# Four output banks behind attention, the last expert by blocks of tokens, and a four-block normalization in one instruction

## The chip, the cores and the metric

The kernel runs on one core of one Trainium2 chip. The metric is the device time of one execution in microseconds (us), inputs in DRAM at the start and the output in DRAM at the end. The engines in the rows are PE (TensorE), DVE (VectorE), ACT (ScalarE), POOL (GpSimd) and SP (SyncE, which issues DMAs here); PSUM is the memory of eight banks that PE writes its sums to.

## The reference

Attention within a window and with 32 global tokens, then a two-layer network over all tokens, then a mixture of eight experts in which each expert takes exactly 272 of the 2176 tokens.

```python
# attention: 4 batches, 8 heads, 512 local + 32 global tokens, 64 per head
# each softmax: exp(s - max) / (sum + 1e-9)
x = attn_out.transpose(0, 2, 1, 3).reshape(2176, 512)
# first network
h = x @ w_in                                        # 512 -> 2048
x = (np.maximum(h, 0) + alpha * np.minimum(h, 0)) @ w_out      # 2048 -> 512
# experts: greedy by the sorted logits, at most 272 tokens each
logits = x @ w_gate
for e in range(8):
    out[mask[e]] = np.maximum(x[mask[e]] @ w1[e], 0) @ w2[e]   # 512 -> 1024 -> 512
```

The weights w_in, w_out, w1 and w2 are used in fp32 accuracy.

## The kernel before

**Numbers.** Nearly all products are made of a fast fp32 format (fp32r in the rows). For accuracy each operand is split into a rounded high half and the rest, and a product is the sum of three: high by high, low by high, high by low. `split` (L73) makes both halves: ACT copies the high one, and DVE or POOL subtracts for the low one. So `g` becomes `ghi` and `glo`, with `glo` on POOL, and an expert's hidden values become `hh` and `hl`. The weights of the first network arrive as 64-bit numbers; `decoding` (L76 to 93) turns them into fp32 on DVE (tile `mag`).

**Stages.** The tokens are in eight chunks of 272 (c = 0 to 7). Features stand on the partitions, tokens along the columns. The hidden 2048 are done in two halves (hf = 0, 1) of eight column blocks (f = 0 to 7).

1. Attention alone, up to about 46 us: PE, DVE and ACT in an order written by hand. A step takes four windows of queries: `scores`, then `norm` (L395 to 401), which adds 1e-9 to the four row sums, takes the reciprocal and scales four blocks of 128 x 128 of P (tile `pr`), then the transposes and the product with v.
2. Attention mixed with the first network, up to about 222 us: the framework's scheduler sets the order. Here `share[0]` is set for a time, and two of the four scalings of a step go to ACT.
3. `gemm` for chunks 3 to 7 of hf = 0, 228 to 357 us, with PE's order as written. In each chunk come eight first products (`gemm1`, 12 matmuls each, tile `h`, epilogue on ACT and at L202 on DVE), then the second product: four output blocks d = 0 to 3, each a sum over eight f with three matmuls for each (L230), tile `y`. A finished bank is copied by ACT to `xd` (L236; two buffers in SBUF), and SP stores it. Beside this the weights of hf = 1 are loaded and decoded.
4. `gemm1b`, the first products of hf = 1, up to about 470 us; then the second products of hf = 1 (L1218) together with the router, which finds each expert's 272 tokens.
5. Eight experts in turn (`slot`): `up` (L1087), `down` (L1105), and `emit`, which transposes the results of the expert before (L1123), copies them to rows and scatters them by token (L1139). The 272 tokens are two blocks of 128 and a rest of 16; the rests of all eight experts are collected in `otail` and scattered at the end as one block of 128.

**What sets the order around the change.** In `gemm` of stage 3 the list at L222 gives PE's order. The banks of `y` come from the pool `pY`, which has two; `gemm1` meanwhile takes its banks `h` in turn from `pH` (two) and, once `odd` is set, from `pO` (two). Between stages 3 and 4 the code puts the router's constants on DVE and POOL (L694 to 779), and behind them `Lrow`, `loadx(0, 1)` and `splitx(0, 1)` (L780 to 782), the load and the split of the first x of stage 4. Each engine runs its own queue in order; the scheduler places instructions of the engines that have no order by hand, so the constants stand in DVE's and POOL's queues in the midst of chunk 7. At the end, `turned` puts the last expert's transposes between the matmuls of `down`, and `emit(E - 1)` follows the last product.

## Time and profile before

| | us |
|---|---|
| three timed runs | 830.79, 832.97, 835.6 |
| their median | 832.97 |
| the profiled execution's own time | 830.71 |
| its span in the trace | 828.933 (shown as 828.9) |
| PE busy | 793.3, 96% of the span |
| DVE, ACT, POOL busy | 472.7, 394.4, 350.6 |

The rows below come from that one profiled execution. In a timeline row stand the start and the duration in us, the engine, the source line, the operation with out<-in, the shapes, the number of like instructions in a row, and in brackets how long the engine had been idle and which instruction released it. Consecutive matmuls overlap in the rows, so the pitch between their starts tells more than the duration of one. The granted clock of PE (PEclk) is a share of the full 2.4 GHz. Idle time of an engine that sets no pace costs nothing.

### The profile page before, as it was taken

How to read it: one execution, taken by the hardware profiler on the slowest of the kernel's cores; microseconds unless marked ns; L12 is line 12 of the kernel's file. 1: busy time of each engine (PE TensorE's matmuls, PEld its weight loads, DVE VectorE, ACT ScalarE, POOL GpSimd, SP SyncE). 2: the span in 40 equal slices, each digit the busy share in tenths (PEclk: the TensorE clock that was granted, in tenths of full speed). 3: DMA queues.
4: the chain of work that ended last, by engine and by line, in shares of the span. 5: the costliest groups of instructions: out<-in, count | busy, mean ns of one | idle time of the engine just before them, and what ended most of it. 6: DMA issues, size and time to landing. Idle time of an engine off the chain costs nothing.

```text
span 828.9 us, 20981 instructions
## 1 busy us (share of the span) xinstructions
PE 793.3 (96%) x8328; PEld 736.8 (89%) x8328; DVE 472.7 (57%) x1681; ACT 394.4 (48%) x982; POOL 350.6 (42%) x305
## 2 busy tenths in 40 slices
PE   7989999999998999899999999999999999999995
PEld 5767778988998999799999999999899999999995
DVE  6899955364267664623334357777677777651120
ACT  6786646564454554323333334342455655454421
POOL 1134322020145443400000465663689989688501
PEclk9999999999998999999999999999999999999998
DMA  9975642631245242003131215424366676466201
GB/s 352 393 286 196 206 151 80 229 130 49 65 151 170 65 129 81 9 21 108 55 108 55 82 53 183 153 58 161 86 203 213 209 219 179 146 193 211 92 27 38
DMA packets 49083, 115.99 MB, mean 140 GB/s; under 512 B 4456, under 2 KB 22312, under 8 KB 46937
## 3 DMA queue, kind: packets, MB, share of 16 engines
q1 hardware_dynamic: 46089, 105.74, 39.4%
q0 software_dynamic: 2896, 8.92, 3.0%
q8 instruction: 65, 1.06, 0.5%
q14 instruction: 33, 0.27, 0.1%
HBM read 96.80 MB, written 17.83 MB: 138 GB/s over the span
## 4 chain that ended last, share of the span: by engine, by line
PE 44%; issue 6%; POOL 3%; DMA 2%; DVE 2%; ACT 1%; POOLq 0%; SPq 0%; ACTq 0%
PE h L196 12%; PE h L1218 10%; PE h L1105 7%; PE h L1087 6%; POOL m L73 2%; DMA raw<-in_moe_w_dram 2%; PE lp L273 1%; PE h L1295 1%; PE pc L923 1%; PE y L230 1%; PE yt L251 1%; PE xt L1067 1%; POOL out_dram L1139 1%; POOL xg L1035 1%; DVE gs L889 0%
## 5 line engine op out<-in xcount | busy, mean ns | idle before, releaser
L196 PE MATMUL h<-xh,win 128*128 128x272 f32 x768 | 161.6, 298 | 2.8 <-ACT win L72 1.2
L73 POOL TENSOR_TENSOR m<-raw,m 128x1024 fp32r<-128x1024 f32 x64 | 152.2, 2398 | 17.3 <-ACT m L72 12.8
L196 PEld LDWEIGHTS h<-xh,win 128*128 128x128 f32 x768 | 125.0, 189 | 11.9 <-issue 4.2
L230 PE MATMUL y<-ghi,wout 128*128 128x272 f32 x512 | 112.6, 303 | 6.7 <-ACT xd L236 2.9
L73 POOL TENSOR_TENSOR glo<-g,ghi 128x272 fp32r<-128x272 f32 x64 | 54.5, 856 | 137.1 <-ACT ghi L72 127.0
L196 PE MATMUL h<-xl,win 128*128 128x272 f32 x384 | 111.3, 290 | 0.0
L73 POOL TENSOR_TENSOR gr<-gb,gr 128x272 fp32r<-128x272 f32 x64 | 47.9, 784 | 148.0 <-ACT gr L72 147.5
L1105 PE MATMUL h<-hh,m 128*128 128x272 f32 x512 | 103.8, 294 | 0.0
L1087 PE MATMUL h<-xsh,m 128*128 128x272 f32 x512 | 103.1, 293 | 0.7 <-DVE hl L1093 0.7
L230 PEld LDWEIGHTS y<-ghi,wout 128*128 128x128 f32 x512 | 85.3, 193 | 13.0 <-issue 3.6
L1218 PE MATMUL h<-gr,wout 128*128 128x272 f32 x672 | 95.1, 294 | 0.0
L201 ACT ACTIVATE neg<-h 128x272 f32<-128x272 f32 x128 | 50.4, 395 | 81.1 <-PE h L196 79.0
L1218 PEld LDWEIGHTS h<-gr,wout 128*128 128x128 f32 x672 | 87.0, 189 | 0.4 <-ACT gr L72 0.4
L72 ACT CAST m<-raw 128x1024 fp32r<-128x1024 f32 x64 | 65.9, 1049 | 41.6 <-DMA raw<-in_moe_w_dram 40.9
L1105 PEld LDWEIGHTS h<-hh,m 128*128 128x128 f32 x512 | 81.5, 188 | 1.5 <-issue 1.5
L1087 PEld LDWEIGHTS h<-xsh,m 128*128 128x128 f32 x512 | 81.6, 188 | 0.9 <-DVE hl L1093 0.9
L230 PE MATMUL y<-glo,wout 128*128 128x272 f32 x256 | 75.5, 296 | 2.8 <-POOL glo L73 2.8
L1105 PE MATMUL h<-hl,m 128*128 128x272 f32 x256 | 75.3, 294 | 0.0
L1087 PE MATMUL h<-xsl,m 128*128 128x272 f32 x256 | 73.9, 292 | 0.0
L196 PEld LDWEIGHTS h<-xl,win 128*128 128x128 f32 x384 | 72.9, 190 | 0.4 <-DVE xl L73 0.4
L202 DVE SCALAR_TENSOR_TENSOR g<-neg,al,h 128x272 f32<-128x272 f32 x64 | 35.7, 560 | 59.1 <-ACT neg L201 51.0
L389 ACT ACTIVATE pr<-sc,mx 128x128 f32<-128x128 f32 x128 | 49.9, 392 | 31.2 <-DVE mx L387 31.2
(262 smaller groups left out, 1538.7 us busy)
## 6 DMA issues: line engine op xcount, KB each, us to landing
raw<-in_moe_w_dram SPq DMA_DIRECT2D x64, 512.0 KB, 3.9
vv<-in_v_dram SPq DMA_DIRECT2D x16, 1024.0 KB, 5.9
qk<-in_qk_dram SPq DMA_DIRECT2D x14, 720.0 KB, 8.4
raw<-in_moe_w_in_dram SPq DMA_DIRECT2D x16, 512.0 KB, 7.6
raw<-in_moe_w_out_dram SPq DMA_DIRECT2D x16, 512.0 KB, 5.9
xs<-xb SPq DMA_DIRECT2D x16, 272.0 KB, 6.9
xpart<-xd SPq DMA_DIRECT2D x32, 136.0 KB, 2.2
xb<-xs SPq DMA_DIRECT2D x8, 544.0 KB
```

The lines of the kernel that those rows point to most:

```text
L72: a = A.copy(hi, src)
L73: return a, (lo_eng or V).tensor_tensor(lo, src, hi.bitcast(F32), op=OP.subtract)
L196: T.matmul(ps, wi[:, w, k, fs], x[:, k], start=i == 0, stop=i == 3 * KD - 1)
L201: A.activation(out=neg, in_=ps, func=AF.Relu, scale=-1.0)
L202: epi[0] = V.scalar_tensor_tensor(g, neg, al1[:, hf * KH + f:hf * KH + f + 1], ps, op0=OP.mult, op1=OP.add)
L230: T.matmul(ps, wo[:, w, f, ds_], x[:, f], start=f == 0 and i == 0, stop=f == KH - 1 and i == 2)
L251: T.transpose(t[:, k * 128:(k + 1) * 128], xo[:, k, a:b], ident)
L273: T.matmul(lp[r:r + 32], w, x, start=n < 4, stop=n >= LT - 4)
L389: A.activation(out=d["pr", j][:, ii], in_=sc, func=AF.Exp, bias=d["mx", j][:, ii:ii + 1], scale=-1.0, accum_out=d["sm", j][:, ii:ii + 1])
L1087: T.matmul(ps, d["w1"][:, w, kk, f * 128:(f + 1) * 128], x[:, kk], start=kk == 0 and i == 0, stop=kk == KD - 1 and i == 2)
L1105: T.matmul(ps, d["w2"][:, w, f, ms], x[:, f], start=i == 0, stop=i == 3 * K3 - 1)
L1218: T.matmul(ps[j], wo[:, w, f, ds_], x, start=f == 0 and a == 0, stop=f == KH - 1 and a == 2)
```

## The change

It has three parts; a move of code (1b) goes with the first.

1. **Banks.** In `gemm`, once `odd` is set (chunks 3 to 7), each of the four output blocks has a bank of its own: d = 0 and 1 from `pY` as before, d = 2 from `pH`, d = 3 from `odd[0]`. All four blocks are summed over f = 0 to 5, and then all four over f = 6 and 7. Before, only d = 0 and 1 were split in this way, and d = 2 and 3 followed whole in the same two banks. In 1b `splitx` also returns its DVE instruction, and `Lrow`, `loadx(0, 1)` and `splitx(0, 1)` stand ahead of the router's constants, which are issued under `tc.issue_after` of that split.
2. **The last expert.** Its second product is made by `by_row`: the hidden values are the stationary operand, the weights the moving one, so that tokens stand on the partitions of the sum, two blocks of 128 tokens and 24 matmuls of 512 columns each. The last 16 tokens are done in plain fp32, with weights `m2f` loaded for them alone and 32 columns of hidden values copied by ACT in `up` (tile `otl`), on four strips of 32 rows that a further matmul with `pick` sums up. No transposes follow. The rests of experts 0 to 6 are emitted with expert 6.
3. **Normalization.** In `norm` the four scalings are one two-operand instruction of 128 x 512, with the reciprocals broadcast; where `share[0]` is set, it takes two blocks, and ACT takes two as before.

```diff
...
-        split(xh, xl, X[c, hf][0] if hf else XB[c // CPB][:, :, (c % CPB) * CH:(c % CPB + 1) * CH])
+        st = split(xh, xl, X[c, hf][0] if hf else XB[c // CPB][:, :, (c % CPB) * CH:(c % CPB + 1) * CH])
         X[c, hf] += [xh, xl]
+        return st[1]
...
-    ybank = [pY, "y"]
...
         if (c + 1, hf) in X:
             splitx(c + 1, hf)
         ys = {}
-        for d, fs in [(0, range(KH - 2)), (1, range(KH - 2)), (0, range(KH - 2, KH)), (1, range(KH - 2, KH))] + [
-                (d, range(KH)) for d in range(2, KD)]:
+        most, rest = range(KH - 2), range(KH - 2, KH)
+        if odd:
+            parts2 = [(d, x) for x in (most, rest) for d in range(KD)]
+        else:
+            parts2 = [(d, x) for x in (most, rest) for d in range(2)] + [(d, range(KH)) for d in range(2, KD)]
+        for d, fs in parts2:
             if d not in ys:
-                ys[d] = ybank[0].tile([128, CH], F32, name="y", tag=ybank[1])
+                pool, tag = (pY, "y") if d < 2 or not odd else (pH, "h1") if d == 2 else odd[0]
+                ys[d] = pool.tile([128, CH], F32, name="y", tag=tag)
             ps = ys[d]
             ds_ = slice(d * 128, (d + 1) * 128)
             for f in fs:
...
             sm = G[p]["sm", j]
             V.tensor_scalar(sm, sm, 1e-9, None, op0=OP.add)
             V.reciprocal(sm, sm)
-            for ii in range(4):
-                x, r = G[p]["pr", j][:, ii], sm[:, ii:ii + 1]
-                if ii % 2 and share[0]:
-                    A.mul(x, x, r)
-                else:
-                    at_norm[p, j] = V.tensor_scalar(x, x, r, None, op0=OP.mult)
+            pr = G[p]["pr", j]
+            own = slice(0, 4, 2 if share[0] else 1)
+            x = pr[:, own]
+            at_norm[p, j] = V.tensor_tensor(x, x, sm[:, own].unsqueeze(2).to_broadcast(list(x.shape)), op=OP.mult)
+            if share[0]:
+                for ii in (1, 3):
+                    A.mul(pr[:, ii], pr[:, ii], sm[:, ii:ii + 1])
 
         def ptrans(p, j):
             d = G[p]
...
-        ybank[:] = [p4, "h4"]
...
+        Lrow = gx2.tile([128, LR], F32, name="Lrow")
+        loadx(0, 1)
+        quiet = ExitStack()
+        quiet.enter_context(tc.issue_after(splitx(0, 1).ins))
...
             P.memset(vas[i], 0.0)
             sbs.append(rc_.tile([128, NP, 32], BF, name=f"sbs{i}"))
             P.memset(sbs[i], 0.0)
-        Lrow = gx2.tile([128, LR], F32, name="Lrow")
-        loadx(0, 1)
-        splitx(0, 1)
+        quiet.close()
...
                                 yield 0.113
                 if kks[-1] == KD - 1:
                     A.activation(out=hh[:, f], in_=ps, func=AF.Relu)
+                    if k == E - 1:
+                        A.activation(out=d["o"][:, f], in_=ps[:, CAP - 32:], func=AF.Relu)
                     V.scalar_tensor_tensor(hl[:, f], ps, 0.0, hh[:, f].bitcast(F32), op0=OP.max, op1=OP.subtract)
                     yield 0.113
...
                     i += 1
                     if i < 3 * K3:
                         yield 0.113
-            if k < E - 1:
-                A.copy(d["o"][:, m], ps)
-            else:
-                A.copy(d["o"][:, m, :256], ps[:, :256])
-                V.tensor_copy(tail["o"][:, m, 16 * k:], ps[:, 256:])
+            A.copy(d["o"][:, m], ps)
 
         scat = []
 
-        def turned(k, m):
-            d = SLOT[k]
-            for q, (a, b) in enumerate(SEG):
-                if m == 0:
-                    pool, tag = ((px, "tx"), (pm, "sm"), (pm, "sm"))[q]
-                    d["t", q] = pool.tile([128, DM], F32, name="ox", tag=tag)
-                T.transpose(d["t", q][:, m * 128:(m + 1) * 128], tail["o"][:, m] if q == 2 else d["o"][:, m, a:b], ident)
+        def scatter(rows, ids):
+            st = P.indirect_dma_start(
+                out=out, out_offset=bass.IndirectOffsetOnAxis(ap=ids, axis=0), in_=rows, in_offset=None)
+            for o in scat:
+                tc.declare_no_dep(st.ins, o.ins, reason="rows of other tokens")
+            scat.append(st)
 
         def emit(k):
             d = SLOT[k]
             orow = sl.tile([128, 3, DM], F32, name="orow")
-            if k < E - 1:
-                A.copy(tail["o"][:, :, 16 * k:16 * k + 16], d["o"][:, :, 256:])
-            for q, (a, b) in enumerate(SEG[:3 if k == E - 1 else 2]):
-                if ("t", q) in d:
-                    t = d["t", q]
-                else:
+            A.copy(tail["o"][:, :, 16 * k:16 * k + 16], d["o"][:, :, 256:])
+            for q, (a, b) in enumerate(SEG[:3 if k == E - 2 else 2]):
+                n = 16 * (E - 1) if q == 2 else 128
+                t = px.tile([128, DM], F32, name="ox", tag="tx")
+                for m in range(KD):
+                    T.transpose(t[:n, m * 128:(m + 1) * 128], tail["o"][:, m] if q == 2 else d["o"][:, m, a:b], ident)
+                A.copy(orow[:n, q], t[:n])
+                scatter(orow[:n, q], TID[:n] if q == 2 else IDS[:, k, q:q + 1])
+                yield 0.5
+
+        def by_row(k):
+            d = SLOT[k]
+            pick = sl.tile([128, 16], F32, name="pick")
+            V.tensor_reduce(pick, ident.rearrange("p (g c) -> p c g", c=32)[:, 16:], axis=AX.X, op=OP.add)
+            orow = sl.tile([128, 3, DM], F32, name="orow")
+            part = d["o"][:, K3:].rearrange("p a b -> p (a b)")
+            terms = [(w, f, x) for f in range(K3) for w, x in ((0, d["h"][0]), (0, d["h"][1]), (1, d["h"][0]))]
+
+            def rows(q, pool, tag):
+                a, b = SEG[q]
+                ps = pool.tile([128, DM], F32, name="ox", tag=tag)
+                for i, (w, f, x) in enumerate(terms):
+                    T.matmul(ps, x[:, f, a:b], d["w2"][:, w, f], start=i == 0, stop=i == len(terms) - 1)
+                    yield 0.22
+                A.copy(orow[:, q], ps)
+                scatter(orow[:, q], IDS[:, k, q:q + 1])
+
+            yield from rows(0, pH, "h1")
+            ps = p4.tile([128, DM], F32, name="ox", tag="h4")
+            for f in range(K3):
+                r = 32 * (f % 4)
+                T.matmul(ps[r:r + 32], d["o"][:, f], d["w2f"][:, f], start=f < 4, stop=f >= K3 - 4)
+            A.copy(part, ps)
+            for i, x in enumerate(rows(1, pH, "h1")):
+                if i == 6:
                     t = px.tile([128, DM], F32, name="ox", tag="tx")
-                    for m in range(KD):
-                        T.transpose(t[:, m * 128:(m + 1) * 128], d["o"][:, m, a:b], ident)
-                (V.tensor_copy if ("t", q) in d and q == 1 else A.copy)(orow[:, q], t)
-                ids = TID if q == 2 else IDS[:, k, q:q + 1]
-                st = P.indirect_dma_start(
-                    out=out, out_offset=bass.IndirectOffsetOnAxis(ap=ids, axis=0), in_=orow[:, q], in_offset=None)
-                for o in scat:
-                    tc.declare_no_dep(st.ins, o.ins, reason="rows of other tokens")
-                scat.append(st)
-                yield 0.5
+                    T.matmul(t[:16], pick, part, start=True, stop=True)
+                    V.tensor_copy(orow[:16, 2], t[:16])
+                    scatter(orow[:16, 2], IDS[:16, k, 2:3])
+                yield x
 
         def slot(k):
             d = SLOT[k]
             d["h"] = (sl.tile([128, K3, CAP], F32R, name="hh"), sl.tile([128, K3, CAP], F32R, name="hl"))
             em = emit(k - 1) if k else iter(())
+            if k == E - 1:
+                d["o"] = sl.tile([128, K3 + DM // 32, 32], F32, name="otl", tag="ot")
             f = 0
             if k == 0:
                 yield from up(k, (0, 1), range(KD - 1), (0, 2))
...
                 if f % 2 == 0:
                     yield next(em, 0)
             d["up"] = True
-            d["o"] = sl.tile([128, KD, CAP], F32, name="ot")
+            if k == E - 2:
+                SLOT[k + 1]["w2f"] = wa.tile([128, K3, DM], F32, name="m2f", tag="wa1")
+                w2e = w2[bass.ds(SLOT[k + 1]["er"], 1)].rearrange("e (k p) f -> p (e k) f", p=128)
+                nc.sync.dma_start(out=SLOT[k + 1]["w2f"], in_=w2e)
+            if k < E - 1:
+                d["o"] = sl.tile([128, KD, CAP], F32, name="ot")
             if k == 0:
-                tail["o"] = sl.tile([128, KD, 128], F32, name="otail", bufs=1)
+                tail["o"] = sl.tile([128, KD, 16 * (E - 1)], F32, name="otail", bufs=1)
+            if k == E - 1:
+                yield from by_row(k)
+                return
             for m in range(KD):
-                for i, x in enumerate(down(k, m)):
-                    if k == E - 1 and m and i == 15:
-                        turned(k, m - 1)
-                    yield x
+                yield from down(k, m)
                 yield 0.113
-            if k == E - 1:
-                turned(k, KD - 1)
...
-        for _ in emit(E - 1):
-            pass
```

PE's order in chunk 3 of stage 3, before, where the first two blocks' sums over f = 0 to 5 end (`y_3911` is d = 1, `y_3882` d = 0, `wout` the weights):

```order
L230 MATMUL y_3911<-ghi_3595,wout_77 128x272 x2
L230 MATMUL y_3911<-glo_3596,wout_77 128x272
L230 MATMUL y_3911<-ghi_3595,wout_77 128x272
L230 MATMUL y_3882<-ghi_3595,wout_77 128x272
L230 MATMUL y_3882<-glo_3596,wout_77 128x272
L230 MATMUL y_3882<-ghi_3595,wout_77 128x272 x2
L230 MATMUL y_3882<-glo_3596,wout_77 128x272
L230 MATMUL y_3882<-ghi_3595,wout_77 128x272
L230 MATMUL y_3911<-ghi_3595,wout_77 128x272
L230 MATMUL y_3911<-glo_3596,wout_77 128x272
```

And after (`y_3821` is d = 1, `y_3840` d = 2):

```order
L235 MATMUL y_3821<-glo_3509,wout_77 128x272
L235 MATMUL y_3821<-ghi_3508,wout_77 128x272 x2
L235 MATMUL y_3821<-glo_3509,wout_77 128x272
L235 MATMUL y_3821<-ghi_3508,wout_77 128x272
L235 MATMUL y_3840<-ghi_3508,wout_77 128x272
L235 MATMUL y_3840<-glo_3509,wout_77 128x272
L235 MATMUL y_3840<-ghi_3508,wout_77 128x272 x2
L235 MATMUL y_3840<-glo_3509,wout_77 128x272
L235 MATMUL y_3840<-ghi_3508,wout_77 128x272 x2
```

Behind f = 5 of d = 1 came f = 6 and 7 of d = 0; now f = 0 of d = 2 comes there.

DVE's order in chunk 7, before, ahead of an epilogue at L202 (`fr`, `home`, `fr_b`, `ones`, `pq_f`, `cols` and `jt` are constants of the router):

```order
L697 TENSOR_SCALAR late<-fr,ipf 128x128
L713 CAST home<-fr 128x17
L720 CAST pq_f<-pq_i 128x2
L724 TENSOR_SCALAR fr_b<-fr 128x128
L733 MEMSET ones 128x128
L735 MEMSET one_c 128x34
L745 TENSOR_SCALAR jt_5362<-j_5360 128x64
L715 TENSOR_SCALAR home<-fr 128x16
L722 TENSOR_SCALAR own<-cols,pq_f 128x24
L202 SCALAR_TENSOR_TENSOR g<-neg,al_70,h_5130 128x272
```

And after (`xl` is the low half of the first x of stage 4, `ipf` and `cols` the first of those constants):

```order
L147 TENSOR_REDUCE wop<-wt 128x4x8
L1351 MEMSET yr 1x512
L837 MEMSET late_pos 128x3
L202 SCALAR_TENSOR_TENSOR g<-neg,al_70,h_5040 128x272
L202 SCALAR_TENSOR_TENSOR g<-neg,al_70,h_5065 128x272
L73 TENSOR_TENSOR xl<-xb,xh 128x1088
L702 CAST ipf<-ip 128x1
L720 CAST cols<-fr 128x24
L722 CAST home<-fr 128x17
L726 TENSOR_SCALAR pq_i<-ip 128x1
```

The constants stood ahead of the epilogue; now the two epilogues and the split of x are ahead of the constants.

PE's order at the end of the kernel, before (`m_11343` is the last expert's w2, `hh` and `hl` the halves of its hidden values, `ot` and `otail` results to be transposed with `ident`):

```order
L1105 MATMUL h_11859<-hl,m_11343 128x272
L1105 MATMUL h_11859<-hh,m_11343 128x272 x2
L1123 MATMUL ox<-ident,ot 128x128 x2
L1123 MATMUL ox<-ident,otail 128x128
L1105 MATMUL h_11859<-hl,m_11343 128x272
L1105 MATMUL h_11859<-hh,m_11343 128x272 x2
L1105 MATMUL h_11859<-hl,m_11343 128x272
L1105 MATMUL h_11859<-hh,m_11343 128x272 x2
L1105 MATMUL h_11859<-hl,m_11343 128x272
L1105 MATMUL h_11859<-hh,m_11343 128x272
L1123 MATMUL ox<-ident,ot 128x128 x2
L1123 MATMUL ox<-ident,otail 128x128
```

And after, at the seam between the two blocks of tokens (`m_11253` is the last expert's w2):

```order
L1154 MATMUL ox<-m_11253,hl 128x512
L1154 MATMUL ox<-m_11253,hh 128x512
L1163 MATMUL ox<-m2f,otl 32x512 x8
L1154 MATMUL ox<-m_11253,hh 128x512
L1154 MATMUL ox<-m_11253,hl 128x512
L1154 MATMUL ox<-m_11253,hh 128x512 x2
L1154 MATMUL ox<-m_11253,hl 128x512
L1154 MATMUL ox<-m_11253,hh 128x512 x2
L1168 MATMUL ox<-otl,pick 16x512
L1154 MATMUL ox<-m_11253,hl 128x512
```

The transposes between and behind the products are gone; the strips of the last 16 tokens stand between the two blocks, and PE's last instruction is a product.

## Rows read from the trace of the kernel before

**Rows 1.** The page: busy us of each engine, share, instructions.

```profile
PE 793.3 (96%) x8328; PEld 736.8 (89%) x8328; DVE 472.7 (57%) x1681; ACT 394.4 (48%) x982; POOL 350.6 (42%) x305
```

**Rows 2.** Timeline of PE, second products of chunks 3 to 6.

```profile
230.70 0.39 PE L230 MATMUL y<-glo,wout 128*128 128x272 f32 x1 [0.40 <-POOL glo L73]
...
252.98 0.29 PE L230 MATMUL y<-ghi,wout 128*128 128x272 f32 x1
...
259.63 0.40 PE L230 MATMUL y<-glo,wout 128*128 128x272 f32 x1 [1.45 <-POOL glo L73]
...
262.30 0.59 PE L230 MATMUL y<-ghi,wout 128*128 128x272 f32 x1 [1.39 <-ACT xd L236]
...
290.80 0.39 PE L230 MATMUL y<-ghi,wout 128*128 128x272 f32 x1 [0.81 <-ACT xd L236]
...
319.71 0.39 PE L230 MATMUL y<-ghi,wout 128*128 128x272 f32 x1 [0.68 <-ACT xd L236]
```

**Rows 3.** Stretches: window, us, each engine's busy us (instructions), PEclk, DMA, GB/s.

```profile
60.00:80.00 20.00, 18.43 (x261) 14.18 (x254) 19.76 (x52) 13.29 (x39) 8.69 (x9) 1.00 0.52 165
260.00:264.00 4.00, 2.61 (x15) 2.39 (x14) 3.86 (x6) 1.85 (x4) 1.27 (x1) 0.67 1.01 307
264.00:268.00 4.00, 4.00 (x20) 4.00 (x19) 0.59 (x1) 0.65 (x2) 1.28 (x1) 0.50 0.88 301
340.00:352.00 12.00, 8.72 (x63) 7.87 (x62) 8.19 (x25) 3.21 (x7) 5.41 (x9) 1.00 0.04 12
780.00:820.00 40.00, 39.54 (x317) 39.13 (x316) 6.26 (x16) 9.27 (x23) 2.25 (x3) 1.00 0.04 14
```

**Rows 4.** Timeline of DVE, POOL and PE in chunk 7.

```profile
338.80 4.80 DVE L202 SCALAR_TENSOR_TENSOR g<-neg,al,h 128x272 f32<-128x272 f32 x1
...
342.48 0.63 POOL L779 MEMSET sbs<- 128x640 bf16 x1
...
344.13 0.76 POOL L73 TENSOR_TENSOR glo<-g,ghi 128x272 fp32r<-128x272 f32 x1 [1.02 <-ACT ghi L72]
...
340.43 0.29 PE L230 MATMUL y<-ghi,wout 128*128 128x272 f32 x1
```

**Rows 5.** Timeline of PE, ACT and POOL from the last expert's second product on.

```profile
806.15 0.29 PE L1105 MATMUL h<-hh,m 128*128 128x272 f32 x1
...
811.20 0.38 PE L1123 MATMUL ox<-ident,ot 128*128 128x128 f32 x2
...
811.45 0.37 PE L1105 MATMUL h<-hl,m 128*128 128x272 f32 x1
...
819.87 0.44 PE L1123 MATMUL ox<-ident,ot 128*128 128x128 f32 x2 [0.46 <-ACT ot L1112]
...
820.23 1.07 ACT L1137 COPY orow<-ox 128x512 f32<-128x512 f32 x2 [0.42 <-PE ox L1123]
...
823.64 0.97 POOL L1139 DMA_INDIRECT out_dram<-orow,TID  x1 [0.30 <-issue]
```

**Rows 6.** Tile `xd`, issue to landing; SP's waits: waited for, total us, times, longest.

```profile
DMA to landing us min/median/max: 1.7/2.2/5.2
...
SPq L79 <- DVE mag L92: 96.5, 23, 8.6
```

**Rows 7.** Plain fp32 on four strips, L140: timeline, then durations in ns, min/median/max.

```profile
332.85 1.07 PE L140 MATMUL wp<-wts,ag 128*32 128x512 f32 x8
...
L140 PE MATMUL wp<-wts,ag x16: 592/604/617, 307.4 to 333.3; 128*32 128x512 f32 x16
```

**Rows 8.** DVE: timeline of three instructions, and durations (ns) of the split of x.

```profile
31.87 0.68 DVE L90 SCALAR_TENSOR_TENSOR mag<-raw,mag 128x512 int32<-128x512 int32 x1
...
32.88 0.88 DVE L401 TENSOR_SCALAR pr<-pr,sm 128x128 f32<-128x128 f32 x4
...
65.81 2.43 DVE L401 TENSOR_SCALAR pr<-pr,sm 128x128 f32<-128x128 f32 x4
...
L73 DVE TENSOR_TENSOR xl<-xb,xh x12: 1278/1294/2376, 41.5 to 434.2; 128x1088 fp32r<-128x1088 f32 x12
```

## The prediction

> **What bounds the kernel now.** I read the busy line first: TensorE (PE) is busy 793.3 of 828.9 us [rows 1]. A faster side engine therefore buys time only where PE waits, so I went through the span in stretches and asked three things of each: does PE wait, for whom, and at which clock. Four places matter for this change.
>
> The first is the second product behind attention: five token chunks, c = 3 to 7. PE waits for the low halves `glo` from POOL and for the copies `xd` on ACT that free a bank: 0.40, 1.45, 1.39, 0.81 and 0.68 us [rows 2]. In chunk 4 the two waits stand 2.7 us apart, and right behind them the granted clock falls to its lower level, 1.2 instead of 2.4 GHz: 0.67 on the average of 260 to 264 us, 0.50 from 264 to 268 [rows 3]. In chunk 7 PE is busy 8.72 of the 12 us from 340 to 352 [rows 3], so 3.28 us are idle, in four waits for `ghi` and `glo` of the last column blocks of h.
>
> The cause of that last loss is one stretch on DVE. The router's constants are queued ahead of the epilogue of f = 5 (L202). That L202 is shown 4.80 us long, to 343.60, and the row of POOL memsets for the router ends at 343.11 [rows 4].
>
> The second place is the end. The last product matmul ends at 819.41, and then come an ACT copy, three transposes, a copy to SBUF, three scatters one behind the other (the last starts at 823.64 and takes 0.97 us) and the landing, up to 828.93: 9.52 us without a product [rows 5].
>
> The third is attention's front, up to about 112 us, where DVE is busy 19.76 of 20 us from 60 to 80 us [rows 3] and PE is fed late. The fourth, from 357 us to the end of the experts, is nearly solid PE and is not touched.
>
> **Part 1, four banks.** In chunks 3 to 7 the pieces now run as d = 0, 1, 2, 3 over f = 0 to 5, then d = 0 to 3 over f = 6 and 7. No matmul is added. A piece over six f is 18 matmuls. A matmul of 272 columns comes every 0.126 us: 40 of them between 806.15 and 811.20 us [rows 5]. So f = 6 is first needed 72 matmuls after the second product begins instead of 36: 9.1 us instead of 4.5. In chunk 4, the worst, that product begins at 252.98 and `glo` of f = 6 lets PE go at 259.63 [rows 2], 6.65 us in. That is inside 9.1, so this wait goes, and so do the smaller ones. The wait for `xd` goes because d = 2 and d = 3 no longer need the banks of d = 0 and 1. Removed: 0.40 + 1.45 + 1.39 + 0.81 + 0.68 = 4.73 us.
>
> With the two waits of chunk 4 gone I expect no fall of the clock there. Its price: 35 matmuls in the 8 us from 260 to 268 [rows 3], of which 1.39 idle; at 0.126 they need 4.4 us, so 8 - 1.39 - 4.4 = 2.2 us.
>
> What is late next: the four `xd` copies now fall 0.76 us apart (6 matmuls) at the chunk's end and share two SBUF buffers, so the third waits for the landing of the first one's store, 1.7 to 5.2 us, median 2.2 [rows 6]. The next chunk's f = 0 and 1 use the other two banks; f = 2 needs that of d = 2 some 24 matmuls, 3.0 us, after the chunk's end. The first copy is done about 1.9 us before that end, so at the median landing the third starts 0.3 us behind the end, in time; at the longest it starts 3.3 us behind it, and with its own 0.4 or so (two copies of twice the width take 1.07 [rows 5]) PE loses 0.7. I put 0.5 us for all five chunks, bounds 0 and 4.
>
> **Part 1b, the constants.** The diff also puts the router's constants on DVE behind the split of the next x, which itself stands behind f = 5 and 6. Then L202 of f = 5 runs at once. But the POOL memsets keep their place ahead of `glo` of f = 5: they end at 343.1, a `glo` takes 0.76 [rows 4], so it is there at 343.9. PE needs it 17 matmuls into the second product, which begins at 340.43 [rows 4]: at 342.5. A wait of 1.4 us is left of the 3.28, a gain of 1.9. Should L202 itself be what POOL holds up, the gain is nothing.
>
> Part 1 in sum: 4.73 + 2.2 + 1.9 - 0.5 = 8.3 us, bounds 3 and 10.
>
> **Part 2, the last expert.** Before: 96 matmuls and nine of the transposes, from 806.15 to 819.41, 13.26 us. After: two blocks of 24 matmuls of 512 columns, 8 plain fp32 matmuls of 512 columns on strips of 32 rows for the last 16 tokens, and one that sums the strips. No row has a 512-column matmul of the fast format. From below it takes its 512 columns at 2.4 GHz, 0.213 us; from above 0.126 x 512/272 = 0.237. I take 0.226: 0.126 us are 302 cycles at the full clock, 30 more than the columns, and that remainder is more likely one per instruction. 48 x 0.226 = 10.8 us. Four plain fp32 matmuls of the same shape on four strips (L140, two instructions each) take 1.07 us [rows 7]: two rounds are 2.1. The summing matmul is one such alone: between a quarter of 1.07 and all of it; one instruction alone is shown as 0.604 [rows 7] and it has two, so I take 0.9. Sum 13.8, 0.55 us more; from 0.7 less to 1.1 more. The tail rows of experts 0 to 6 are now transposed inside the last up product: three transposes take 0.25 us of the stream [rows 5], four about 0.35.
>
> The end gets shorter. Behind the last matmul: a copy of about 0.55 us (two take 1.07), 0.30 to the scatter, 0.97, and from the end of the last scatter's issue to the span's end 4.32 as before [rows 5]: 6.2 instead of 9.52, 3.3 less. The two other scatters go out during the 4 us of matmuls ahead of that. Eight small ACT copies and the 2 MB load of the plain weights go beside the last products: ACT is busy 9.27 of 40 us there and DMA moves 14 GB/s [rows 3]; without that cover the load would cost several us, but it has over 25. Net: 3.3 - 0.55 - 0.35 = 2.4 us, bounds 1.6 and 3.9.
>
> **Part 3, normalization.** Where nothing disturbs DVE, the four instructions of 128 columns take 0.88 us; a two-tensor instruction of 512 columns takes 0.68 [rows 8]. So 0.2 us is saved per step. Some ten steps stand up to 46 us and some six up to 112, where DVE sets the pace: at most 16 x 0.2 = 3.2. The first ones wait for loads and for ACT's exp too, so I take 1.2. Later steps lie under solid PE and give nothing. The scheduler also shuffles PE, ACT and DVE a little between 46 and 120 us, for which I have no row: bounds 4 lost and 5 gained.
>
> The four small instructions cost 0.2 us each, mostly whatever their width. The Trainium skill ("VectorE: DVE Perf Modes", section "The perf-mode tier table") gives fp32 tensor_scalar in SBUF twice the rate of tensor_tensor, which speaks against this edit. By that rule alone the edit would be a loss; the 0.68 us row does not bear it out at this width.
>
> **Sum.** 8.3 + 2.4 + 1.2 = 11.9 us off the profiled execution's 830.71 us: 818.8. That execution lies at the lower end of the three timed runs (830.79 to 835.6, median 832.97), so I add about half of the 2.3 us between them: **820 us**.
>
> **The rivals.**
> A, the copies take the place of the wait: the four bunched `xd` hold ACT, and with it the next chunk's epilogues, about 1 us in each of five chunks. For it: landings up to 5.2 us. Against: the median of 2.2. Part 1 gives 3.8 instead of 8.3: 824.5.
> B, normalization gets slower. A two-tensor instruction may wait for POOL: the split of x takes 1.278 us at best and 2.376 at worst [rows 8]. At 1.1 us more in each of the six steps up to 112 us, 6.6 are lost and 1.2 not gained: 828. Against: the four small ones lose as much already, 2.43 instead of 0.88 us at 65.81 [rows 8]. Half the rate without any waiting, 1.76 us instead of 0.88 in those six steps, would be 826.5; that is what the page's rule makes of it.
> C, slower than before: the store of the first `xd` stands behind a weight load on SP's queue, which waits for decoding on DVE, at the longest 8.6 us [rows 6]. ACT then stands still, and the four banks with it; the next f = 2 comes 9.3 us late. Twice that and two falls of the clock at 2.2: 820 + 23 = 843. It decides from about 6 us of lateness in two chunks on. Against: in the new order ACT's casts of the weights that free those loads stand ahead of the copies.
> D, the change doesn't do what it says: the clock falls in chunk 4 anyway, or the waits only move; 826 to 830.
>
> **How the numbers follow.** The forecast has 0.64 (with a range of its own of 813 to 826), A 0.14, B 0.10, D 0.08, C 0.04. The range 812 to 829 takes in the bounds of parts 2 and 3, A and most of B and D, and leaves C out. Half a per cent, about what a measurement here can tell from no change, is 4.2 us: below 828.8 is faster. Faster 0.86, same 0.10, slower 0.04.
>
> **What will show it.** Right: no PE wait for `xd` and none over 0.2 us for `glo` in chunks 3 to 6, a clock of 1.00 throughout them, one wait of 1 to 2 us in chunk 7; about 0.226 us between the 512-column matmuls and 6.2 us from the last of them to the end. Wrong: ACT's `xd` waiting for DMA with PE idle in f = 2 of the next chunk; a normalization that takes over 0.9 us on average; or new waits of PE between 46 and 120 us, where only the schedule has moved.

## The result, and the profile after

The changed kernel takes 825.5 us (median of 4 runs, 822.52 to 826.96) against 832.25 us before (4 runs): a ratio of 0.9905, with a 95% interval of 0.9878 to 0.9932. A second set, 6 runs against 11, gives 0.9887 (0.9865 to 0.9909). So it is faster, as forecast and inside the range of 812 to 829, but by 7 to 10 us and not by the 12 that lie between the forecast 820 and the median before. The 825.5 also lies nearer to rival A's 824.5 than to the forecast.

The profiled execution took 825.84 us, its span is 824.1. The page's busy line, to be read against [rows 1]: PE does as much as before; DVE lost 15.6 us that the time does not show.

```profile
PE 792.1 (96%) x8290; PEld 732.8 (89%) x8290; DVE 457.1 (55%) x1588; ACT 394.0 (48%) x988; POOL 354.8 (43%) x306
```

**Behind attention.** Timeline of PE, every wait of over 0.12 us from the second product of chunk 3 to that of chunk 7; these rows answer to [rows 2, 4].

```profile
234.29 0.39 PE L235 MATMUL y<-glo,wout 128*128 128x272 f32 x1 [0.33 <-POOL glo L73]
...
274.14 0.39 PE L196 MATMUL h<-xh,win 128*128 128x272 f32 x1 [2.07 <-ACT xd L241]
...
286.66 0.40 PE L235 MATMUL y<-glo,wout 128*128 128x272 f32 x1 [1.09 <-POOL glo L73]
...
343.43 0.39 PE L235 MATMUL y<-glo,wout 128*128 128x272 f32 x1 [1.46 <-POOL glo L73]
```

Of the waits in [rows 2] four are gone and one of 0.33 us stays. Two are new, 2.07 us for a copy `xd` ahead of the next chunk's f = 2, and 1.09 us for `glo` in chunk 5. Chunk 7 keeps one wait of 1.46 us. The stretches that answer to [rows 3] (window, us, busy us of each engine, PEclk, DMA share, GB/s):

```profile
260.00:264.00 4.00, 4.00 (x34) 4.00 (x33) 4.00 (x5) 1.64 (x4) 3.88 (x3) 1.00 0.42 131
264.00:268.00 4.00, 4.00 (x34) 4.00 (x33) 3.86 (x6) 0.76 (x2) 1.36 (x2) 1.00 0.88 269
340.00:352.00 12.00, 10.54 (x84) 10.32 (x83) 6.30 (x34) 2.19 (x4) 4.88 (x8) 1.00 0.01 1
```

In chunk 4 the clock stays up: 68 matmuls in the 8 us in which 35 ran before.

**The end.** Timeline of PE, ACT and POOL from the last expert's second product on, answering to [rows 5]:

```profile
803.38 0.40 PE L1154 MATMUL ox<-m,hh 128*128 128x512 f32 x1
...
808.70 0.40 PE L1154 MATMUL ox<-m,hh 128*128 128x512 f32 x1
809.03 1.92 PE L1163 MATMUL ox<-m2f,otl 128*32 128x512 f32 x16
810.88 0.50 PE L1154 MATMUL ox<-m,hh 128*128 128x512 f32 x1
...
812.70 1.03 PE L1168 MATMUL ox<-otl,pick 128*16 128x512 f32 x2
813.66 0.50 PE L1154 MATMUL ox<-m,hl 128*128 128x512 f32 x1
...
817.45 0.40 PE L1154 MATMUL ox<-m,hh 128*128 128x512 f32 x1
...
817.88 0.58 ACT L1156 COPY orow<-ox 128x512 f32<-128x512 f32 x1 [6.25 <-PE ox L1154]
...
818.74 0.98 POOL L1123 DMA_INDIRECT out_dram<-orow,IDS  x1 [3.17 <-ACT orow L1156]
```

Twenty-four matmuls of 512 columns take from 803.38 to 808.70, 0.231 us from start to start. The last ends at 817.85, and 6.22 us later the kernel ends; before it was 9.52 us. The product itself takes 14.47 us instead of 13.26.

**The front.** Here the profile after is slower: the second product of chunk 3 begins at 231.78 instead of 228.12 us. Whether the change did that was the first question for the experiments.

To compare executions I cut each profile at the same four points: the start of the second product of chunk 3, that of chunk 7, the last matmul into `y`, and the end of the span. The last column is the time at the lower clock before 120 us, summed over stretches of 4 us as (1 - PEclk) x 2 x 4. The names are those of the experiments below.

| kernel | chunk 3 begins | to chunk 7 | chunk 7 | to the end | low clock before 120 |
|---|---|---|---|---|---|
| before | 228.12 | 112.31 | 16.58 | 471.9 | 3.4 |
| changed | 231.78 | 108.01 | 13.97 | 470.3 | 13.6 |
| before_again | 228.94 | 110.97 | 16.61 | 473.1 | 3.4 |
| after_again | 232.16 | 107.95 | 13.96 | 469.9 | 13.6 |
| no_norm | 230.80 | 107.72 | 14.00 | 471.6 | 10.3 |
| no_banks | 230.56 | 111.42 | 14.24 | 469.5 | 10.2 |
| no_row | 230.01 | 107.98 | 13.96 | 472.3 | 10.3 |
| no_const | 229.30 | 107.82 | 16.37 | 471.6 | 3.4 |
| xd4 | 228.75 | 105.74 | 13.97 | 471.5 | 6.9 |
| mem_late | 229.83 | 107.98 | 12.23 | 471.8 | 10.3 |
| xd4_mem | 227.85 | 105.66 | 12.24 | 472.1 | 3.4 |
| phase1 | 230.90 | 107.93 | 12.24 | 470.9 | 10.2 |
| phase2 | 232.15 | 107.14 | 12.23 | 469.7 | 13.6 |
| xd4_mem_old_norm | 230.03 | 105.79 | 12.24 | 470.0 | 6.9 |

The second and third columns of times answer each question on their part to a few tenths of a us, as long as the clock stays up there; in chunk 7 it fell for 3.4 us in before_again and in no_const. The first and the last move by 4 and 3 us between executions of like code.

The runs come in sets, each on a chip of its own together with runs of before, and the medians of before differ: 834.79 us with after_again, no_norm, no_banks and no_row; 833.12 with no_const, xd4, mem_late and xd4_mem; 833.83 with phase1 and phase2; 832.89 with xd4_mem_old_norm. Inside a set I compare times, between sets the ratios to before. The changed kernel's is 0.9887 (0.9905 in the first, smaller set), and the 95% interval of each ratio reaches 0.002 to 0.004, or 2 to 3 us, to either side.

### The profile page after: what moved, and what is told of

Same layout as the page of the kernel before. It is cut to its first block, busy times and chain, and to the rows that moved or that the text cites. A ratio compares the mean times of both kernels' runs of the same rounds, so it can differ in the third digit from the quotient of the medians.

```text
span 824.1 us, 20827 instructions
## 1 busy us (share of the span) xinstructions
PE 792.1 (96%) x8290; PEld 732.8 (89%) x8290; DVE 457.1 (55%) x1588; ACT 394.0 (48%) x988; POOL 354.8 (43%) x306
## 3 DMA queue, kind: packets, MB, share of 16 engines
q8 instruction: 65, 1.06, 0.5%
## 4 chain that ended last, share of the span: by engine, by line
PE 73%; DVE 8%; POOL 5%; issue 5%; DMA 5%; ACT 3%; SPq 0%; POOLq 0%; DVEq 0%; ACTq 0%
PE h L196 20%; PE h L1250 10%; PE y L235 10%; PE h L1094 8%; PE h L1114 7%; PE o L424 3%; DMA raw<-in_moe_w_dram 2%; POOL m L73 2%; PE s L386 2%; PE go L473 2%; PE lp L278 1%; PE t L413 1%; PE h L1327 1%; DVE mag L92 1%; PE pc L930 1%
## 5 line engine op out<-in xcount | busy, mean ns | idle before, releaser
L235 PE MATMUL y<-ghi,wout 128*128 128x272 f32 x512 | 108.6, 298 | 3.1 <-POOL wout L73 2.2
L1114 PE MATMUL h<-hh,m 128*128 128x272 f32 x448 | 91.4, 295 | 0.0
L235 PEld LDWEIGHTS y<-ghi,wout 128*128 128x128 f32 x512 | 82.9, 189 | 8.1 <-issue 3.8
L1114 PEld LDWEIGHTS h<-hh,m 128*128 128x128 f32 x448 | 71.4, 189 | 0.9 <-issue 0.9
L1114 PE MATMUL h<-hl,m 128*128 128x272 f32 x224 | 65.9, 294 | 0.0
L202 DVE SCALAR_TENSOR_TENSOR g<-neg,al,h 128x272 f32<-128x272 f32 x64 | 31.5, 493 | 58.8 <-ACT neg L201 51.9
L202 DVE SCALAR_TENSOR_TENSOR gb<-neg,al,h 128x272 f32<-128x272 f32 x64 | 31.2, 495 | 58.7 <-ACT neg L201 58.7
```

What stands on the lines that cost most here:

```text
L202: epi[0] = V.scalar_tensor_tensor(g, neg, al1[:, hf * KH + f:hf * KH + f + 1], ps, op0=OP.mult, op1=OP.add)
L235: T.matmul(ps, wo[:, w, f, ds_], x[:, f], start=f == 0 and i == 0, stop=f == KH - 1 and i == 2)
L1114: T.matmul(ps, d["w2"][:, w, f, ms], x[:, f], start=i == 0, stop=i == 3 * K3 - 1)
```

## The experiments

### The two kernels once more

The changed kernel, unedited:

> The changed kernel once more, unedited. In the first profile of it the second product of chunk 3 begins 3.67 us later than before (231.91 against 228.24 us). Theory 1, this is chance of one execution (a load of qk that landed 1.65 us later, and falls of the clock whose place is not fixed): the start of chunk 3 is now elsewhere by a microsecond or more, 228 to 231, and the time is 822 to 826. Theory 2, it comes from the new order of instructions between 46 and 120 us: chunk 3 begins at 231.5 to 232.5 again, with falls of the clock at about 58 to 64 and 92 to 97 us.

It took 824.88 us (6 runs), and chunk 3 began at 232.16 us with the clock low for as long as in the first profile. Taken alone this looked like theory 2. The other kernels with the same code up to there say otherwise: they begin chunk 3 anywhere from 227.85 to 232.16, by and large later where the clock was low for longer (last column of the table). The same stretch in two of them, after_again and then xd4_mem:

```profile
60.00:64.00 4.00, 4.00 (x49) 3.51 (x48) 3.81 (x8) 2.60 (x8) 2.02 (x3) 0.50 0.80 326
64.00:68.00 4.00, 4.00 (x30) 3.31 (x29) 2.46 (x5) 0.91 (x2) 1.61 (x1) 0.65 0.41 133
```

```profile
60.00:64.00 4.00, 4.00 (x54) 3.13 (x52) 3.93 (x7) 2.05 (x7) 2.85 (x3) 1.00 0.80 295
64.00:68.00 4.00, 4.00 (x48) 3.45 (x44) 3.55 (x13) 3.50 (x12) 2.05 (x2) 1.00 0.46 144
```

The fall of the clock around 60 us comes in some executions and not in others. The kernel before, unedited, for a second profile:

> The kernel before once more, unedited, for a second profile. Its first profiled execution (830.71 us) lies under the median of all its runs, and there the second product of chunk 3 begins at 228.12 us; in the seven other kernels with the same code up to that point it begins anywhere from 227.85 to 232.16, later where the clock is low for longer between 46 and 100 us. Theory 1, that spread is chance of the execution in the kernel before as well: here chunk 3 begins later by up to 4 us if the clock is low for more than the 3.4 us (weighted) of the first profile, and the time from there to the end stays within 1.5 us of 600.8. Theory 2, the kernel before always reaches chunk 3 at about 228.1.

One run: 831.42 us, chunk 3 at 228.94 with 3.4 us of low clock, and 600.7 us from there to the end. So the rest is steady, but both profiles of before show a good front, and their times lie under the medians of its other runs, 832.25 to 834.79. Theory 1 is not shown by this run; it is borne out by no_norm below, which has the old front, shows the early fall as well (0.50 from 52 to 56 us) and begins chunk 3 at 230.80.

### The four banks

Two banks again, the constants left where the change put them:

```diff
-        if odd:
-            parts2 = [(d, x) for x in (most, rest) for d in range(KD)]
-        else:
-            parts2 = [(d, x) for x in (most, rest) for d in range(2)] + [(d, range(KH)) for d in range(2, KD)]
+        parts2 = [(d, x) for x in (most, rest) for d in range(2)] + [(d, range(KH)) for d in range(2, KD)]
...
-                pool, tag = (pY, "y") if d < 2 or not odd else (pH, "h1") if d == 2 else odd[0]
-                ys[d] = pool.tile([128, CH], F32, name="y", tag=tag)
+                ys[d] = pY.tile([128, CH], F32, name="y", tag="y")
```

> The changed kernel with the second product of chunks 3 to 7 in two banks as before; the router's constants stay behind the split of x. From the start of chunk 3's second product to that of chunk 7's the kernel before takes 112.4 us and the changed one 108.0. Theory 1, four banks alone make that difference: 4.4 us slower than the changed kernel, about 830, with the clock at 0.50 again for some 5 us in chunk 4, behind two waits of 1.4 us. Rival, the fall of the clock in chunk 4 is chance and not of the waits: the clock stays up, and the kernel is 1.5 us slower, 827.

827.64 us, 2.8 more than the changed kernel, and 3.4 more from chunk 3 to chunk 7, where 4.4 were expected. Its timeline of PE and the stretches of chunk 4:

```profile
261.98 0.39 PE L231 MATMUL y<-glo,wout 128*128 128x272 f32 x1 [1.44 <-POOL glo L73]
264.65 0.60 PE L231 MATMUL y<-ghi,wout 128*128 128x272 f32 x1 [1.41 <-ACT xd L237]
```

```profile
260.00:264.00 4.00, 1.80 (x13) 1.36 (x11) 3.93 (x5) 0.98 (x2) 1.92 (x2) 1.00 0.57 172
264.00:268.00 4.00, 3.35 (x15) 3.35 (x16) 2.83 (x3) 2.19 (x5) 1.61 (x2) 0.57 1.07 375
```

The two waits are back and so is the fall of the clock behind them, here for 3.4 us. Chunk 4 (from its second product to that of chunk 5) takes 29.0 us; it was 30.2 in the first profile of before with 6.8 us of low clock, and 28.9 in the second with 3.4. So 3.4 us at the lower clock cost 1.3 here. The fall came behind these two waits in all three profiles that have them. In the eleven profiles with four banks the clock fell in chunk 4 once, behind a wait of 2.06 us; seven others with one wait of 1.06 to 2.07 us in that chunk show no fall there. So the two waits brought it about here, and a single one mostly did not.

### The constants

The constants ahead of the split of x again:

```diff
-        Lrow = gx2.tile([128, LR], F32, name="Lrow")
-        loadx(0, 1)
-        quiet = ExitStack()
-        quiet.enter_context(tc.issue_after(splitx(0, 1).ins))
...
-        quiet.close()
+        Lrow = gx2.tile([128, LR], F32, name="Lrow")
+        loadx(0, 1)
+        splitx(0, 1)
```

> The changed kernel with the router's constants ahead of the split of x again, as before. The second product of chunk 7 takes 16.33 us before and 13.84 in the changed kernel. Theory 1, the place of the constants on DVE makes that difference: 2.5 us slower than the changed kernel, 828, and PE waits for ghi of f = 5. Rival, the four banks alone shorten chunk 7 because f = 6 and 7 are needed later: 0 to 0.8 us slower.

Chunk 7 takes 16.37 us, 2.4 more, and PE waits for `ghi` again:

```profile
340.80 0.39 PE L235 MATMUL y<-ghi,wout 128*128 128x272 f32 x1 [1.63 <-ACT ghi L72]
341.64 0.39 PE L235 MATMUL y<-glo,wout 128*128 128x272 f32 x1 [0.45 <-POOL glo L73]
```

The clock fell here too (the same columns as in the stretches above):

```profile
340.00:344.00 4.00, 2.75 (x13) 2.54 (x14) 3.86 (x20) 2.02 (x4) 1.52 (x2) 0.77 0.00 1
344.00:348.00 4.00, 4.00 (x28) 4.00 (x28) 1.01 (x4) 0.42 (x1) 0.77 (x1) 0.81 0.00 0
```

So the 2.4 us are not all waiting. Without waits chunk 7 takes 12.23 us (mem_late, below). In the changed kernel and in the first profile of before, where the clock stays up, a wait costs its row and 0.27 us more (13.97 less 12.23 and 1.46; 16.58 less 12.23 and 3.27, over four waits). By that estimate the two waits of no_const make 0.9 of its 2.4 us and the fall of the clock 1.5. Of waiting alone the rival's 0 to 0.8 us is thus not far off: with four banks the two waits at f = 7 (0.75 and 0.45 us in the first profile of before) are gone whatever the constants do. What speaks for theory 1 is no_banks: two banks, the constants moved, a full clock in chunk 7, and 14.24 us there, 2.3 less than in the first profile of before, whose clock is full there as well.

The median, 825.52 us, is 0.9913 of before's (0.9887 to 0.9940), 2.2 us more than the changed kernel by ratio where 2.5 were expected, but the two intervals overlap. Medians of six to nine runs do not resolve 2 us of this kernel, and the stretches do.

### The last expert

`up`, `down`, `turned`, `emit` and `slot` as before, with the closing loop over `emit(E - 1)`:

```diff
...
-            if k == E - 1:
-                yield from by_row(k)
-                return
             for m in range(KD):
-                yield from down(k, m)
+                for i, x in enumerate(down(k, m)):
+                    if k == E - 1 and m and i == 15:
+                        turned(k, m - 1)
+                    yield x
...
```

> The changed kernel with the last expert's second product, transposes and scatters as before. In the two profiles the stretch from the end of the logits' transposes (473.28 and 470.00 us) to the end is 355.65 us before and 354.10 in the changed kernel: 1.55 us slower than the changed kernel, about 827. Rival, as forecast, 2.4 us slower: 828.

825.68 us, 0.8 more, with chunk 3 at 230.01. From the last `y` to the end it takes 472.3 us; the three profiles with the old end take 471.9 to 473.1 there, the eleven with the new one 469.5 to 472.1, mean 470.8. The difference of the means is 1.6 us, near the 1.55 expected. Shorter stretches say it without that spread. From the start of the last expert's second product to the end it takes 22.78 or 22.79 us in the three profiles with the old end and 20.68 to 20.70 in the eleven with the new one, 2.09 less. The up product ahead of it, which now has the four transposes of the rests inside, takes 13.42 us instead of 12.99. It starts here, in the first profile of before and then of the changed kernel:

```profile
793.16 0.30 PE L1087 MATMUL h<-xsh,m 128*128 128x272 f32 x1
```

```profile
789.96 0.30 PE L1094 MATMUL h<-xsh,m 128*128 128x272 f32 x1
```

So 1.66 us are left, 0.7 less than forecast; the rival falls.

### The normalization

The four scalings again:

```diff
-            pr = G[p]["pr", j]
-            own = slice(0, 4, 2 if share[0] else 1)
-            x = pr[:, own]
-            at_norm[p, j] = V.tensor_tensor(x, x, sm[:, own].unsqueeze(2).to_broadcast(list(x.shape)), op=OP.mult)
-            if share[0]:
-                for ii in (1, 3):
-                    A.mul(pr[:, ii], pr[:, ii], sm[:, ii:ii + 1])
+            for ii in range(4):
+                x, r = G[p]["pr", j][:, ii], sm[:, ii:ii + 1]
+                if ii % 2 and share[0]:
+                    A.mul(x, x, r)
+                else:
+                    at_norm[p, j] = V.tensor_scalar(x, x, r, None, op0=OP.mult)
```

> The changed kernel with the four scalings of the normalization as before. Theory 1, the new instruction takes 0.69 instead of 0.88 us and saves some 0.2 us in each step that DVE paces: this kernel is 0.5 to 2 us slower than the changed one, 826 to 827.5. Theory 2, the edit costs more by the order it brings between 46 and 230 us than it saves: this kernel is 2 to 4 us faster, 821.5 to 823.5, and chunk 3's second product begins at 228 to 229 us.

825.16 us: 0.3 more, and neither theory's number. DVE spends 35.1 us on the 122 scalings here and 21.3 on the one-instruction form in the changed kernel (groups of instructions by line and shape, of no_norm and then of the changed kernel: count | busy us, mean ns | idle before):

```profile
L406 DVE TENSOR_SCALAR pr<-pr,sm 128x128 f32<-128x128 f32 x122 | 35.1, 348 | 0.9
```

```profile
L404 DVE TENSOR_TENSOR pr<-pr,sm 128x512 f32<-128x512 f32 x29 | 20.0, 689 | 0.7
L404 DVE TENSOR_TENSOR pr<-pr,sm 128x256 f32<-128x256 f32 x3 | 1.3, 420 | 0.1
```

Why 14 us off DVE bring so little shows between 88 and 93 us. DVE, POOL and PE of the changed kernel there, and POOL in the kernel before at the same split of w_out:

```profile
89.24 0.68 DVE L404 TENSOR_TENSOR pr<-pr,sm 128x512 f32<-128x512 f32 x1
89.84 1.28 DVE L73 TENSOR_TENSOR xl<-xb,xh 128x1088 fp32r<-128x1088 f32 x1
91.05 0.68 DVE L90 SCALAR_TENSOR_TENSOR mag<-raw,mag 128x512 int32<-128x512 int32 x1
...
88.86 4.00 POOL L73 TENSOR_TENSOR wout<-mag,wout 128x512 fp32r<-128x512 f32 x1 [3.30 <-ACT wout L72]
...
92.91 0.59 PE L235 MATMUL y<-ghi,wout 128*128 128x272 f32 x1 [2.21 <-POOL wout L73]
```

```profile
87.06 2.22 POOL L73 TENSOR_TENSOR wout<-mag,wout 128x512 fp32r<-128x512 f32 x1
```

Three two-operand instructions stand in a row on DVE (behind one of a single operand, L88, 0.42 us from 88.91), and beside them POOL's split takes 4.00 us instead of some 1.3. PE waits 2.21 us for it. All ten profiles with the one instruction show this split at 3.99 to 4.01 us and the wait at 2.20 or 2.21; none of the four with the old form does. There the four scalings stretch instead, to 2.4 us as in [rows 8], and POOL's split takes 1.27 or 2.2. The Trainium skill ("SBUF — State Buffer", section "Who interferes with whom") says that a DVE instruction with two inputs in SBUF contends with a POOL instruction that reads SBUF, that the ports they share are an exclusive lock, and that the order of issue decides who blocks. These rows agree on the contention. On who waits they differ from case to case: at 89 us it is POOL, whose row begins 0.05 us ahead of L88, which is too close to tell the order, while in chunk 4 of the same profile POOL begins 0.18 us ahead of the split of x and the split takes 2.37 us instead of 1.28:

```profile
260.89 1.40 POOL L73 TENSOR_TENSOR win<-mag,win 128x512 fp32r<-128x512 f32 x1
...
261.07 2.37 DVE L73 TENSOR_TENSOR xl<-xb,xh 128x1088 fp32r<-128x1088 f32 x1
```

A last run asked what is left at equal clock: the version with both improvements below, with the four scalings:

> Four buffers xd, the constants on POOL late, and the four scalings of the normalization as before. From the tenth normalization (at about 46 us) to the one at about 128 us the profiles so far take, with the four scalings: 82.94 and 82.76 us where the clock is low for a weighted 3.4 us, 84.32 with 10.3 us; with the one instruction: 82.05 and 82.08 with 3.4 us, 83.2 to 83.9 with 10.2 or 10.3. Theory 1, at an equal clock the one instruction saves 0.75 us there: this kernel takes 82.8 with 3.4 us of low clock, 83.6 with 6.9, 84.3 with 10.3, and it is about 0.8 us slower than the version with the one instruction, 820. Rival, the two sets only look apart by chance: 82.1, 83.0 or 83.6, and 819.3.

It takes 84.05 us from the tenth normalization to the one at about 130 us, with 6.9 us of low clock; the one-instruction form took 82.97 in xd4 with as much. So the saving is about 0.8 us at equal clock (0.4 to 1.1 by these pairs). The median, 819.97, is 0.9833 of before's where xd4_mem's is 0.9852, with intervals that overlap; that decides nothing. Six of the ten profiles with the one instruction had 6.8 or 6.9 us of low clock around that wait of 2.2 us, the four with the old form 3.4 each. What the edit saves on DVE it may thus give back through the clock; whether it does so on average stays open.

### What was late next

Four buffers for `xd` in chunks 3 to 7, in a pool of their own:

```diff
...
-            xd = gx.tile([128, CH], F32, name="xd", bufs=2)
+            xd = gx.tile([128, CH], F32, name="xd", bufs=2) if not odd else xdp[0].tile([128, CH], F32, name="xd")
...
```

> The changed kernel with four instead of two buffers xd in chunks 3 to 7. In the changed kernel the third copy xd of chunk 4 waits 1.62 us for the store of the first to land, and PE 2.07 us for that copy; in chunk 5 PE waits 1.09 us for glo. Theory 1, the two buffers cause the first wait and, through late epilogues, the second: both go, 2 to 3 us faster than the changed kernel, 822.5 to 823.5. Rival, POOL with its splits of the weights paces chunk 5: the first wait moves into one for glo, and the time falls by under 1 us.

821.78 us, a ratio of 0.9862, by which it is 2.1 us below the changed kernel; chunks 3 to 7 take 2.2 less. ACT at the end of chunk 4 in the changed kernel, and then in xd4:

```profile
267.86 0.68 ACT L83 ACTIVATE mag<-raw 128x512 f32<-128x512 f32 x1 [1.40 <-POOL win L73]
269.13 0.62 ACT L72 CAST win<-mag 128x512 fp32r<-128x512 f32 x1 [0.59 <-DVE mag L92]
269.66 0.38 ACT L241 COPY xd<-y 128x272 f32<-128x272 f32 x1
271.15 0.67 ACT L83 ACTIVATE mag<-raw 128x512 f32<-128x512 f32 x1 [1.11 <-POOL win L73]
271.72 0.36 ACT L241 COPY xd<-y 128x272 f32<-128x272 f32 x1
273.70 0.77 ACT L241 COPY xd<-y 128x272 f32<-128x272 f32 x2 [1.62 <-DMA xpart<-xd]
```

```profile
267.69 0.67 ACT L83 ACTIVATE mag<-raw 128x512 f32<-128x512 f32 x1 [1.11 <-POOL win L73]
268.26 0.94 ACT L242 COPY xd<-y 128x272 f32<-128x272 f32 x3
```

ACT's queue holds two steps of a weight's decoding ahead of the first copy and a third ahead of the second, and all three wait for other engines. The first copy starts at 269.66 although its bank was full about 3 us earlier (second product begun at 256.82, 78 matmuls of 0.126 us). Only then come the landing of its store and the third copy. With four buffers the last three copies run through. The wait for `glo` in chunk 5 stays at 1.07 us, so the late copies were not its cause: theory 1 is right on the first wait and wrong on the second.

POOL's constants behind the last `glo` of chunk 7 (`low` holds that split's POOL instruction):

```diff
...
+        quiet.enter_context(tc.issue_after(low[0].ins))
```

> The changed kernel with the router's constants on POOL queued behind the last low half of chunk 7 too. Theory 1, the eight memsets ahead of glo of f = 5 cause PE's wait of 1.46 us in chunk 7: it goes, 1.4 us faster than the changed kernel, 824. Rival, the epilogue on DVE is as late as glo: PE waits for ghi in its place, and the time stays within 0.4 us.

822.85 us, a ratio of 0.9874 (1.1 us below the changed kernel), and chunk 7 takes 12.23 instead of 13.97 us. POOL there, where the last `glo` is now ahead of the constants:

```profile
339.85 1.56 POOL L73 TENSOR_TENSOR glo<-g,ghi 128x272 fp32r<-128x272 f32 x1 [0.99 <-ACT ghi L72]
341.37 0.13 POOL L702 IOTA ip<- 128x1 int32 x1
```

No wait of over 0.12 us is left on PE in that chunk: 96 matmuls at 0.126 us are 12.1. Both edits together:

> Both: four buffers xd, and the router's constants on POOL behind the last low half of chunk 7. Theory 1: the two gains add, 3.4 to 4.4 us faster than the changed kernel, 821 to 822, and no wait of PE over 0.5 us is left between 232 us and the end of chunk 7. Rival: only the memsets' part comes, 824.

819.34 us (6 runs, 817.77 to 825.83), 2.4 less than xd4 and 3.5 less than mem_late in the same set, and the lowest median here. The ratio to before is 0.9852 (0.9817 to 0.9887), by which it is 2.9 us below the changed kernel. In the stretches the two gains add: 2.3 us from chunk 3 to 7, 1.7 in chunk 7. Against the expectation one wait of over 0.5 us is left, in chunk 5; POOL and PE there:

```profile
278.35 1.29 POOL L73 TENSOR_TENSOR wout<-mag,wout 128x512 fp32r<-128x512 f32 x1
279.59 1.50 POOL L73 TENSOR_TENSOR glo<-g,ghi 128x272 fp32r<-128x272 f32 x2
...
280.41 0.39 PE L237 MATMUL y<-glo,wout 128*128 128x272 f32 x1 [1.09 <-POOL glo L73]
```

A split of w_out stands ahead of the `glo` that PE waits for. Two runs put the parts of the weights in at other steps (both on top of xd4_mem; phase2 has `== 2`):

```diff
-                if n % 7 == 0 and parts:
+                if n % 7 == 1 and parts:
```

> Four buffers xd, the constants on POOL behind the last low half, and the parts of the weights of hf = 1 put in six steps earlier (every seventh step, beginning with the first). In the last version without this, PE still waits 1.09 us for glo of f = 5 in chunk 5, and on POOL a split of w_out of 1.29 us ends right ahead of that glo. Theory 1, that split's place in the queue makes the wait: in the new order no weight split stands between glo of f = 2 and glo of f = 6 in chunk 5, the wait goes, and no other takes its place: 1.1 us less, 818 to 818.5. Rival, POOL has too much to do in these chunks whatever the order: a wait for glo of the same size stands in another chunk, and the time stays at 819 to 819.5.

> The same with the parts put in five steps earlier: on POOL a weight split then stands ahead of glo of f = 3 and of f = 6 in chunk 5, none right ahead of f = 5. Theory 1: the wait for glo of f = 5 goes as well, 818 to 818.5. Rival: it moves to f = 6 or to chunk 6, 819 to 819.5.

821.33 and 822.67 us, ratios of 0.9848 and 0.9867, which cannot be told from xd4_mem's 0.9852; but 107.93 and 107.14 us from chunk 3 to 7 instead of 105.66. The wait in chunk 5 goes in both, and others come, of phase1 and then of phase2:

```profile
247.50 0.39 PE L198 MATMUL h<-xh,win 128*128 128x272 f32 x1 [0.77 <-ACT xd L243]
...
273.82 0.39 PE L198 MATMUL h<-xh,win 128*128 128x272 f32 x1 [1.06 <-ACT xd L243]
...
302.19 1.07 PE L140 MATMUL wp<-wts,ag 128*32 128x512 f32 x8 [0.72 <-ACT wts L135]
```

```profile
261.43 0.39 PE L237 MATMUL y<-glo,wout 128*128 128x272 f32 x1 [1.26 <-POOL glo L73]
```

Theory 1 falls in both: other waits took the place of the one that went, and these chunks became longer. Of the rivals, phase2's holds, with 1.26 us for `glo` in chunk 4. In phase1 it holds in part: the new waits are mainly for ACT, for the copies `xd` and for `wts`, and not for POOL. That these chunks have too much side work for any order is not shown; two other orders moved the wait.

## Why the prediction was right, and where it was too high

**Banks, the waits.** Forecast 4.73 us removed; 4.33 went. The 0.40 us in chunk 3 stayed as 0.33, since it was put down to f = 6 by mistake: 230.70 less the 0.40 of waiting is 2.2 us behind the start, 17 matmuls, which is `glo` of f = 5, and four banks do not move that. In chunk 4 the matmul that waits for `glo` is the 41st, so it is f = 7 and not f = 6; that wait goes all the same.

**Banks, the clock.** Forecast 2.2. Its mechanism is borne out by no_banks. The price was 2.6 in the first profile of before (6.8 us low at 1.3 for each 3.4), 1.3 in the second.

**Banks, what is late next.** This is the step that failed: 0.5 us for all five chunks, where 2.07 came in one, and 1.09 for `glo` in chunk 5. The mechanism is that of rival A and of that step, late copies that wait for a store to land. What was wrong is the time of the first copy, put at 1.9 us ahead of the chunk's end from PE's side alone. Against rival C the prediction said that ACT's casts of the weights stand ahead of the copies; that very order holds the copies up. Together the three terms gave 6.4; measured from chunk 3 to 7 are 4.3 against the first profile of before and 3.0 against the second.

**Constants.** Forecast 1.9, from 3.28 us of waiting to 1.4. Against the first profile of before the waits fall by 1.8 and chunk 7 by 2.6, since each wait costs some 0.27 us more than its row. That part was counted for the constants alone, but the waits at f = 7 go by four banks as well as by the constants, and in before_again and no_const a fall of the clock, 1.5 us in no_const, stands in the place of waits. The wait left was forecast at 1.4 us behind the POOL memsets and is 1.46; mem_late shows them to be its cause.

**The last expert.** Forecast 2.4, measured 1.66 by the rows (1.6 by the means). The end is 3.30 shorter as forecast (3.3), the transposes inside the last up product cost 0.43 (0.35). The product is 1.21 us longer instead of 0.55: 0.231 us for a matmul of 512 columns and not 0.226, 1.85 us for the strips, 0.96 for the summing matmul, and about 0.1 where each format follows the other.

**Normalization.** Forecast 1.2 in the front. The instruction takes 0.69 instead of 0.88 as read from [rows 8], so the rule of the Trainium skill that the prediction weighed ("VectorE: DVE Perf Modes", section "The perf-mode tier table") does not decide at 128 columns an instruction. Rival B named the right pair but the wrong loser: POOL's split waits, not the normalization. At equal clock some 0.8 us are left. The prediction had no term of its own for what that wait of POOL does to PE, 2.21 us.

**The sum.** 3.0 to 4.3 from the banks, 2.6 in chunk 7, 1.7 from the end and 0 to 1 from the normalization make 7 to 9.6 us, where 11.9 were forecast and 7 to 10 measured. To that comes the step from the profile to the median: half of 2.3 us was added, while both profiles of before had a front with little low clock, up to 4 us ahead of the later ones, so the whole gap was due. With 8.5 and 2.3 the sum would have given 824.5; that is a sum made with the result known. The direction and most of the mechanisms were right. That the time lay inside the range owes something to the range's width.
